# Low parts of the first MLP's w_out: from VectorE to GpSimd, in two pieces

## The chip, the cores and the metric

The kernel runs on one core of one Trainium2 chip. The core has TensorE (matrix multiplication; PE in the profile, its weight loads PEld), VectorE (DVE), ScalarE (ACT), GpSimd (POOL) and SyncE (SP), which here issues the DMAs. They have a queue of instructions each and wait for one another through semaphores. The metric is device time in microseconds, the median of the runs.

## What is computed

Attention with a causal window of 128 over 4 batches, 8 heads, 576 positions and a head dimension of 64; then two MLPs over all 2304 tokens, with a model dimension of 512 and a hidden one of 2048:

```python
scores = where(mask, scale * q @ k.T - slope * distance, -1e9)
x = softmax(scores) @ v                   # tokens x 512
h = x @ w_in                              # 512 x 2048
g = where(h >= 1, h, where(h <= -1, 0, (h + 1) ** 2 / 4))
x = g @ w_out                             # 2048 x 512
h = x @ w_in2
return (h * clip(h + 3, 0, 6) / 6) @ w_out2
```

## The kernel before, in words

The weights lie in memory as 64-bit floating-point numbers. The kernel loads them as pairs of 32-bit words and makes 32-bit numbers of them itself; q, k and v are 32-bit numbers already.

TensorE multiplies in the type fp32r. To keep more digits, most operands are split: a high part, which is the operand cast to fp32r, and a low part, which is the operand less its high part. A product is then three matmuls (low by high, high by low, high by high). split_hi (L135) and split_lo (L143) make the parts, each on the engine that it is given.

The class Weights (L148) holds an MLP's weights in 16 chunks (KF) of 128 hidden columns. A chunk f holds the w_in half (512 columns: four blocks of the model dimension) and the w_out half (512 columns). For each chunk:

- load issues two DMAs, for w_in and for w_out, into raw.
- conv1 (L173): ScalarE makes the tile m from raw (L178, 128x1024) and changes raw in place (L179).
- conv2 (L181): VectorE puts the number together in m: a shift (L185), a combination of sign and rest (L187), an addition (L189).
- conv3 (L191): ScalarE casts m to the high part (L137 in the profile, 128x1024), and VectorE subtracts it from m to make the low part (L144, 128x1024). High and low part lie in hl, with the size [128, 2, 2, 512]: part, then w_in or w_out, then column. hl takes the place of raw.

The tile m comes from the pool conv, which has three buffers. Tiles for an MLP block's results (o1) share them.

conv_tick (L199) takes one step: conv2 and conv3 of chunk n-1, then conv1 of chunk n. The first two ticks lie at the end of the first attention unit; the others are spread over the blocks of the first MLP by the function spread. The tokens are processed in blocks of 256 (the first three) or 384 columns. The order is: block 0 with the first eight chunks (A), block 1 with the same eight, block 0 with the last eight (Z), block 1 with those, and then the other blocks with all sixteen. Between the matmuls of one chunk and the next, the hook places loads, conversions and attention steps. The chunk that a block uses is converted about one chunk ahead in block 0.

For a chunk, Mlp.first (L542) makes h: 12 matmuls with w_in as weights (L549), beginning with w_in's low part. activate (L574) makes g on VectorE, ScalarE and VectorE (L578, L579, L580), casts its high part on ScalarE (L137) and makes its low part on GpSimd (L144, 128x256 for these blocks). Mlp1.second (L585) makes acc from w_out's parts and g: 12 matmuls (L591). It comes two chunks behind (LAG), so that g has time.

The attention's steps stand between these. prep (L293) makes the parts of k on ScalarE and VectorE (kh L303, kl L305) and those of q (qs): in the first three units the high part on GpSimd (L139 in the profile), the low part on GpSimd (L144). Scores are two matmuls (L329), followed by a reduction on VectorE (L350) and an exponential on ScalarE (L353).

The instructions of every engine but SP are put into an order by a planner when the kernel is built: it goes by the order of the program, and by its own estimate of when an instruction can start. SP's order is that of the program. On the chip every queue is worked off in its order.

Of the kernel before, what the change touches and what calls it, by code (L numbers as in the profile page):

```python
# [38 lines left out]
def tile_window_attention_two_mlps(  # L39
# [21 lines left out]
    PIECE = DM  # L61
# [73 lines left out]
    def split_hi(eng, hi, x):  # L135
        if eng == "act":
            nc.scalar.copy(hi, x)  # L137
        elif eng == "pool":
            nc.gpsimd.tensor_scalar(out=hi, in0=x, scalar1=1.0, scalar2=1.0, op0=ALU.mult, op1=ALU.mult)  # L139
        else:  # L140
            engines[eng].tensor_copy(hi, x)

    def split_lo(eng, lo, x, hi):  # L143
        engines[eng].tensor_tensor(out=lo, in0=x, in1=hi.bitcast(F32), op=ALU.subtract)  # L144

    class Weights:  # L148
        def __init__(self, nm, w_in, w_out, pool):
            self.src = {"i": w_in.bitcast(U32), "o": w_out.bitcast(U32)}  # L150
            self.nm, self.pool = nm, pool
            self.raw, self.m, self.hl = {}, {}, {}
            self.n_load = 0
            self.n_conv = 0
# [36 lines left out]
        def conv3(self, f):  # L191
            del self.raw[f]
            m = self.m.pop(f)
            hl = wpool.tile([P, 2, 2, PIECE], F32R, tag=f"w{f}", name=f"w{self.nm}{f}")
            split_hi("act", hl[:, 0], m)
            split_lo("dve", hl[:, 1], m, hl[:, 0])
            self.hl[f] = hl

        def conv_tick(self):  # L199
# [514 lines left out]
    halves = {}  # L714
    thirds = [0, 1, 2]
    W1 = Weights("a", w_in1, w_out1, cpool)
    chunks = Chunks()


# [13 lines left out]
    with ExitStack() as actx:  # L733
        mlp1 = Mlp1(W1, blocks1, rpool, gpool)
        raw = actx.enter_context(tc.tile_pool(name="raw", bufs=2))
# [15 lines left out]
        att.more_loads(1)  # L751
        W1.load()

        n_pre = unit_steps[0] + LAG_D
        for t in range(n_pre):
            att.tick()
            if t % 3 == 0:
                W1.load()
            if t >= n_pre - 2:
                W1.conv_tick()  # L760

        def spread(part, ticks, conv):

            slots = 2 * len(part)
            att0, conv0 = att.t, W1.n_conv

            def hook(f, after):
                k = 2 * (f - part[0]) + after + 1
                W1.load()
                while W1.n_conv < conv0 + min(conv, -(-conv * k // slots)) and W1.conv_tick():  # L770
# [118 lines left out]
```

## Time and profile before

| | before |
|---|---|
| median of 3 runs | 1000.5 us (999.63 to 1001.77) |
| profiled execution | 999.68 us |
| its span, first to last instruction | 997.9 us |
| TensorE matmuls, busy | 968.9 us (97%) |
| TensorE weight loads, busy | 882.8 us (88%) |
| VectorE, busy | 602.9 us (60%) |
| ScalarE, busy | 515.9 us (52%) |
| GpSimd, busy | 259.3 us (26%) |

The shares are means over stages that have different limits: GpSimd has no work after some 530 us, and the first MLP's weights are converted between some 20 and 158 us. A busy matmul row isn't TensorE at its peak, as matmuls overlap and their ends are modelled; the weight loads, one for each matmul, say more. Times in the rows below are counted from the span's start.

### The profile page before, as it was taken

What the parts mean: (1) busy time and instruction counts of PE and PEld (TensorE: products, weight loads), DVE (VectorE), ACT (ScalarE), POOL (GpSimd) and SP (SyncE); (2) the same over time, 40 slices, a digit from 0 to 9 for tenths busy, and PEclk for the clock granted to TensorE, in tenths of its full rate; (3) what the DMA queues carried; (4) which work ended last, traced back from release to release, by engine and by line L of the source; (5) the groups of instructions that cost most, each with busy time, mean ns of one, the idle gap of its engine ahead of it and who ended that gap; (6) DMA issues with size and microseconds to landing.
All of it is one profiled execution on the core that took longest, in us unless ns stands there. A gap on an engine that the chain in (4) does not pass through costs nothing.

```text
span 997.9 us, 16828 instructions
## 1 busy us (share of the span) xinstructions
PE 968.9 (97%) x5748; PEld 882.8 (88%) x5748; DVE 602.9 (60%) x1544; ACT 515.9 (52%) x1260; POOL 259.3 (26%) x403
## 2 busy tenths in 40 slices
PE   7799999999999999999999999999999999999998
PEld 5687888999999998899999999999988888888886
DVE  4889996587678666668764998942242224223222
ACT  5688874567657566656653878522242223222121
POOL 3335454456545555455530000000000000000000
PEclk9899999999999999999999999999999999999999
DMA  5685823223212121222203884000030002001001
GB/s 171 168 258 173 271 66 87 78 67 94 75 42 80 50 80 44 63 59 80 62 12 105 293 277 169 1 1 1 1 106 1 1 1 84 1 1 43 1 1 42
DMA packets 75092, 80.00 MB, mean 80 GB/s; under 512 B 8704, under 2 KB 67072, under 8 KB 75008
## 3 DMA queue, kind: packets, MB, share of 16 engines
q1 hardware_dynamic: 75008, 78.94, 25.8%
q8 instruction: 45, 0.74, 0.3%
q14 instruction: 39, 0.32, 0.1%
HBM read 68.42 MB, written 10.49 MB: 79 GB/s over the span
## 4 chain that ended last, share of the span: by engine, by line
PE 85%; DVE 6%; ACT 4%; issue 2%; DMA 2%; POOL 1%; SPq 0%; ACTq 0%; DVEq 0%; POOLq 0%
PE h L549 37%; PE acc L646 20%; PE acc L591 17%; PE s L329 3%; PE r L466 3%; PE r L411 2%; PE t L380 1%; PE t L381 1%; DVE kl L305 1%; DVE r L578 1%; DMA qr<-qT 1%; ACT p L353 1%; DVE r L580 1%; DVE p L350 1%; DMA vr<-v 1%
## 5 line engine op out<-in xcount | busy, mean ns | idle before, releaser
L549 PE MATMUL h<-x,wa 128*128 128x384 f32 (+1 forms) x1344 | 231.5, 316 | 4.4 <-DVE r L580 2.5
L591 PE MATMUL acc<-g,wa 128*128 128x384 f32 (+1 forms) x1344 | 228.8, 315 | 1.7 <-POOL g L144 1.5
L549 PEld LDWEIGHTS h<-x,wa 128*128 128x128 f32 x1344 | 207.6, 190 | 7.0 <-DVE r L580 4.4
L549 PE MATMUL h<-x,wb 128*128 128x512 f32 (+1 forms) x960 | 210.5, 368 | 0.0
L591 PEld LDWEIGHTS acc<-g,wa 128*128 128x128 f32 x1344 | 206.3, 189 | 4.0 <-POOL g L144 2.2
L646 PE MATMUL acc<-wb,g 128*128 128x512 f32 x864 | 209.4, 390 | 0.0
L549 PEld LDWEIGHTS h<-x,wb 128*128 128x128 f32 x960 | 176.3, 188 | 25.0
L646 PEld LDWEIGHTS acc<-wb,g 128*128 128x128 f32 x864 | 161.7, 188 | 32.3
L636 DVE SCALAR_TENSOR_TENSOR r<-r,h 128x512 f32<-128x512 f32 (+1 forms) x80 | 50.7, 633 | 195.5 <-ACT r L635 195.4
L635 ACT ACTIVATE r<-h 128x512 f32<-128x512 f32 (+1 forms) x80 | 44.4, 556 | 207.9 <-PE h L549 207.8
L137 ACT CAST g<-r 128x384 fp32r<-128x384 f32 (+2 forms) x192 | 98.3, 512 | 69.6 <-DVE r L636 48.7
L144 POOL TENSOR_TENSOR g<-r,g 128x256 fp32r<-128x256 f32 (+1 forms) x96 | 92.0, 958 | 129.2 <-ACT g L137 114.0
L579 ACT ACTIVATE r<-r 128x384 f32<-128x384 f32 (+1 forms) x112 | 53.6, 478 | 93.5 <-DVE r L578 93.3
L353 ACT ACTIVATE p<-p,sm 128x256 f32<-128x256 f32 (+2 forms) x160 | 76.0, 476 | 24.4 <-DVE sm L350 21.6
L144 DVE TENSOR_TENSOR g<-r,g 128x384 fp32r<-128x384 f32 (+1 forms) x96 | 59.9, 624 | 44.7 <-ACT g L137 44.6
L578 DVE TENSOR_SCALAR r<-h 128x384 f32<-128x384 f32 (+1 forms) x112 | 55.5, 496 | 37.4 <-PE h L549 33.2
L144 POOL TENSOR_TENSOR qs<-qr,qs 64x256 fp32r<-64x256 f32 (+3 forms) x88 | 68.8, 781 | 28.4 <-issue 7.5
L580 DVE TENSOR_TENSOR r<-h,r 128x384 f32<-128x384 f32 (+1 forms) x112 | 55.7, 497 | 28.9 <-ACT r L579 28.3
L350 DVE CUSTOM_DVE_ANT_0 p<-s,dist 128x256 f32<-128x256 f32 (+2 forms) x160 | 59.7, 375 | 11.1 <-PE s L329 8.8
L358 POOL TENSOR_SCALAR p<-p,sm 128x256 f32<-128x256 f32 (+1 forms) x104 | 48.1, 463 | 61.7 <-DVE sm L357 37.4
L329 PE MATMUL s<-kh,qs 128*128 128x256 f32 (+2 forms) x160 | 55.0, 347 | 1.8 <-POOL qs L144 1.2
L305 DVE SCALAR_TENSOR_TENSOR kl<-kr,kh 128x256 fp32r<-128x256 f32 (+4 forms) x88 | 51.7, 587 | 7.3 <-ACT kh L303 7.1
(75 smaller groups left out, 1153.5 us busy)
## 6 DMA issues: line engine op xcount, KB each, us to landing
rawa<-w_in SPq DMA_DIRECT2D x16, 512.0 KB, 5.6
rawa<-w_out SPq DMA_DIRECT2D x16, 512.0 KB, 5.1
rawb<-w_in SPq DMA_DIRECT2D x16, 512.0 KB, 3.8
rawb<-w_out SPq DMA_DIRECT2D x16, 512.0 KB, 4.6
kr<-kT SPq DMA_DIRECT2D x80, 64.0 KB, 2.3
out<-o SPq DMA_DIRECT2D x18, 256.0 KB, 2.1
qr<-qT SPq DMA_DIRECT2D x64, 64.0 KB, 2.3
vr<-v SPq DMA_DIRECT2D x24, 128.0 KB, 2.4
```

The costliest lines, as they stand in the source:

```text
L137: nc.scalar.copy(hi, x)
L144: engines[eng].tensor_tensor(out=lo, in0=x, in1=hi.bitcast(F32), op=ALU.subtract)
L305: nc.vector.scalar_tensor_tensor(out=u.kl[:, :nk], in0=u.kr[:, :nk], scalar=unit, in1=u.kh[:, :nk].bitcast(F32), op0=ALU.mult, op1=ALU.sub ...
L329: nc.tensor.matmul(ps[:m, :nk], q[:, qo:qo + m], k[:, ko:ko + nk], start=(w == 0), stop=(w == len(parts) - 1))
L350: nc.vector.tensor_tensor_reduce(out=pt[:m, :nk], in0=ps[:m, :nk], in1=dist[:m, bo:bo + nk], scale=-slopes[u.h], scalar=3.0e38, op0=ALU.ad ...
L353: nc.scalar.activation(out=pt[:m, :nk], in_=pt[:m, :nk], func=AF.Exp, bias=sm[:m, 0:1], scale=-1.0, accum_out=None if u.whole else sm[:m, ...
L549: nc.tensor.matmul(ps[:, :n], self.W.w_in(a, c, f), self.x_chunk(x, b, c, n), start=(k == 0), stop=(k == 3 * KC - 1))
L578: nc.vector.tensor_scalar(out=r[:, :n], in0=ps[:, :n], scalar1=-1.0, scalar2=1.0, op0=ALU.max, op1=ALU.min)
L579: nc.scalar.activation(out=r[:, :n], in_=r[:, :n], func=AF.Square, bias=0.5, scale=0.5)
L580: nc.vector.tensor_tensor(out=r[:, :n], in0=ps[:, :n], in1=r[:, :n], op=ALU.max)
L591: nc.tensor.matmul(acc[i][:, o * n:(o + 1) * n], self.W.w_out(a, f)[:, e * P:(e + 1) * P], g[:, b, :n], start=(first and k == 0 and o == 0 ...
L646: nc.tensor.matmul(acc[t][:, :DM], g[:, b, t * P:(t + 1) * P], self.W.w_out(a, f), start=(first and k == 0), stop=(last and k == 2))
```

## The change

For the first MLP alone (W1.lo_pool = True), conv3 makes the low part in three instructions in place of one. VectorE subtracts only the w_in half, 128x512. GpSimd subtracts the w_out half in two pieces of 128x256. The high part remains one cast on ScalarE. The second MLP's weights are converted as before, and no DMA is changed.

```diff
     class Weights:
+        lo_pool = False
+
         def __init__(self, nm, w_in, w_out, pool):
...
             split_hi("act", hl[:, 0], m)
-            split_lo("dve", hl[:, 1], m, hl[:, 0])
+            if self.lo_pool:
+
+                split_lo("dve", hl[:, 1, 0], m[:, 0], hl[:, 0, 0])
+                for q in range(0, PIECE, PIECE // 2):
+                    cols = slice(q, q + PIECE // 2)
+                    split_lo("pool", hl[:, 1, 1, cols], m[:, 1, cols], hl[:, 0, 1, cols])
+            else:
+                split_lo("dve", hl[:, 1], m, hl[:, 0])
             self.hl[f] = hl
...
     W1 = Weights("a", w_in1, w_out1, cpool)
+    W1.lo_pool = True
     chunks = Chunks()
```

## Rows read from the trace of the kernel before

**Rows 1.** Windows: start:end, length, busy us of each engine (instructions), clock, DMA

```profile
75.00:150.00 75.00, 72.36 (x556) 64.03 (x556) 71.31 (x167) 61.65 (x140) 38.70 (x39) 1.00 0.53 169
175.00:200.00 25.00, 25.00 (x213) 25.00 (x213) 15.00 (x47) 13.59 (x39) 10.90 (x17) 1.00 0.26 78
25.00:160.00 135.00, 124.53 (x921) 108.78 (x920) 123.41 (x301) 106.09 (x249) 61.16 (x64) 0.97 0.59 179
```

**Rows 2.** The chain that ended last, between 75 and 150 us, shares by line

```profile
by line: PE h L549 24.9%; PE acc L591 19.4%; PE r L411 10.6%; issue 5.1%; ACT rawa L179 3.6%; DMA kr<-kT 3.0%; PE s L329 2.9%; PE t L381 2.9%; DMA qr<-qT 2.8%; ACT p L353 2.5%; POOL g L144 2.1%; ACT wa L137 2.0%; PE s L116 1.9%; DVE ma L189
```

**Rows 3.** Groups by line and shape, 25 to 160 us: busy us, mean ns

```profile
L144 DVE TENSOR_TENSOR wa<-ma,wa 128x1024 fp32r<-128x1024 f32 x16 | 20.9, 1304 | 0.9 <-ACT wa L137 0.8
L189 DVE CUSTOM_DVE_ANT_0 ma<-rawa,ma 128x2048 uint16<-128x2048 uint16 x15 | 20.2, 1349 | 0.6 <-ACT rawa L179 0.6
L187 DVE SCALAR_TENSOR_TENSOR ma<-rawa,ma 128x1024 uint32<-128x1024 uint32 x15 | 19.5, 1302 | 0.1
L185 DVE TENSOR_SCALAR ma<-ma 128x1024 uint32<-128x1024 uint32 x15 | 11.8, 786 | 0.8 <-ACT ma L178 0.8
L305 DVE SCALAR_TENSOR_TENSOR kl<-kr,kh 128x448 fp32r<-128x448 f32 x8 | 6.8, 844 | 0.2 <-ACT kh L303 0.2
```

**Rows 4.** The same view, whole span: the second MLP's stage

```profile
L144 DVE TENSOR_TENSOR g<-r,g 128x512 fp32r<-128x512 f32 x48 | 33.2, 692 | 31.0 <-ACT g L137 31.0
...
L144 DVE TENSOR_TENSOR wb<-mb,wb 128x1024 fp32r<-128x1024 f32 x16 | 19.5, 1217 | 0.3 <-ACT wb L137 0.2
L189 DVE CUSTOM_DVE_ANT_0 mb<-rawb,mb 128x2048 uint16<-128x2048 uint16 x16 | 19.5, 1217 | 0.0
L187 DVE SCALAR_TENSOR_TENSOR mb<-rawb,mb 128x1024 uint32<-128x1024 uint32 x16 | 19.4, 1218 | 0.0
...
L185 DVE TENSOR_SCALAR mb<-mb 128x1024 uint32<-128x1024 uint32 x16 | 10.7, 687 | 1.7 <-ACT mb L178 1.6
```

**Rows 5.** Timeline: start, length in us, instruction, [idle before <-releaser]

```profile
40.21 0.62 DVE L305 SCALAR_TENSOR_TENSOR kl<-kr,kh 128x448 fp32r<-128x448 f32 x1
...
52.22 0.87 POOL L144 TENSOR_TENSOR qs<-qr,qs 64x320 fp32r<-64x320 f32 x1
52.26 1.31 DVE L305 SCALAR_TENSOR_TENSOR kl<-kr,kh 128x448 fp32r<-128x448 f32 x1 [0.24 <-ACT kh L303]
...
90.47 2.99 POOL L144 TENSOR_TENSOR qs<-qr,qs 64x192 fp32r<-64x192 f32 x1
```

**Rows 6.** Instructions on the tile g, 25 to 160 us: shortest/median/longest ns

```profile
L144 POOL TENSOR_TENSOR g<-r,g x20: 724/742/1674, 51.0 to 158.9; 128x256 fp32r<-128x256 f32 x20
```

**Rows 7.** Timeline: casts and subtractions of chunks, and a matmul behind one

```profile
22.18 1.04 ACT L137 CAST wa<-ma 128x1024 fp32r<-128x1024 f32 x1 [0.77 <-DVE ma L189]
...
25.27 1.22 DVE L144 TENSOR_TENSOR wa<-ma,wa 128x1024 fp32r<-128x1024 f32 x1
...
94.78 1.22 DVE L144 TENSOR_TENSOR wa<-ma,wa 128x1024 fp32r<-128x1024 f32 x1
...
96.05 1.10 PE L549 MATMUL h<-x,wa 128*128 128x256 f32 x7 [0.60 <-DVE wa L144]
...
154.18 1.05 ACT L137 CAST wa<-ma 128x1024 fp32r<-128x1024 f32 x1 [1.05 <-DVE ma L189]
...
155.25 1.23 DVE L144 TENSOR_TENSOR wa<-ma,wa 128x1024 fp32r<-128x1024 f32 x1
```

**Rows 8.** Timeline: a g on ScalarE and GpSimd, and the next acc

```profile
96.36 0.41 ACT L137 CAST g<-r 128x256 fp32r<-128x256 f32 x1
...
96.91 1.49 POOL L144 TENSOR_TENSOR g<-r,g 128x256 fp32r<-128x256 f32 x1 [3.45 <-ACT g L137]
...
101.94 0.92 PE L591 MATMUL acc<-g,wa 128*128 128x256 f32 x6
```

**Rows 9.** Timeline of ScalarE: a wait for a buffer of m

```profile
136.19 1.17 ACT L178 ACTIVATE ma<-rawa 128x1024 f32<-128x1024 f32 x1 [0.26 <-DVE wa L144]
```

**Rows 10.** Who waited for whom, 25 to 160 us: total us, times, longest

```profile
PE acc L591 <- POOL g L144: 1.5, 3, 0.6
```

## The prediction

> **What bounds the kernel now.** I read four views in turn. First the windows [rows 1]: between 175 and 200 us the weight loads fill the window (25.00 of 25 us), so TensorE sets the time there, and an engine beside it that gets less work would change nothing. Where the first MLP's weights are converted, from 25 to 160 us, it is otherwise. VectorE is busy 71.31 of 75 us between 75 and 150 us, and 123.41 of 135 us over the stretch, while TensorE's weight loads are busy 64.03 of 75 us. So VectorE is the tightest engine there, and TensorE has at most about 11 us to win back between 75 and 150 us. The granted clock of that window is 1.00, so the clock is no term of the sum. GpSimd works 61.16 of 135 us in 64 instructions.
>
> Second, the chain of waits between 75 and 150 us [rows 2]. It runs through TensorE's h and acc for 44% and then through short pieces of ScalarE, VectorE, GpSimd and input DMAs: no engine holds it alone. A microsecond taken off VectorE can shorten the stretch, but not always by a whole one.
>
> Third, the groups of that stretch [rows 3] against the same operations for the second MLP's weights, where GpSimd does nothing [rows 4]. Every conversion operation is dearer in the first place: 1304 against 1217 ns, 1349 against 1217, 1302 against 1218, 786 against 687. Fourth, the timeline shows why [rows 5]: a kl that takes 0.62 us alone took 1.31 us when a GpSimd subtraction had begun 0.04 us earlier, and ended 0.48 us after it; and a GpSimd subtraction took 2.99 us while one VectorE operation with two SBUF inputs followed another. The two engines block each other.
>
> **The change, part by part.** All of it lies between 22 and some 158 us; nothing behind that is edited, and it carries over whatever the stretch gains or loses.
>
> *VectorE loses work.* Sixteen subtractions of 128x1024 become sixteen of 128x512. Without GpSimd beside them these sizes cost 1217 and 692 ns [rows 4], so 0.525 us each goes, 16 x 0.525 = 8.4 us.
>
> *GpSimd gains work.* Thirty-two subtractions of 128x256 with two SBUF inputs. The same shape is its g low part: median 742 ns, shortest 724, longest 1674 [rows 6]; in the mean 997 with what blocks it. So 23.7 us unblocked, 32 us at that mean. GpSimd has 135 - 61 = 74 us without work [rows 1], and the sum fits.
>
> *The two engines collide more.* VectorE's loss to blocking today: 16 x 0.087 + 15 x 0.132 + 15 x 0.084 + 15 x 0.099 = 6.1 us for the conversions [rows 3, 4], and 8 x (0.844 - 0.62) = 1.8 us for the large kl [rows 3, 5]. That is 7.9 us beside 64 GpSimd instructions, 0.123 us for each. Thirty-two more at this rate cost 4.0 us. The new ones are not spread at random, since a piece is released by the same ScalarE cast as VectorE's half. Over the sixteen pairs of cast and subtraction, from 22.18 and 25.27 us to 154.18 and 155.25 us [rows 7], seven subtractions begin within 0.06 us of the cast's end, as the last does (155.23 to 155.25). There VectorE should take the memory first, since a GpSimd subtraction released by a cast begins later than that (after 96.77 at 96.91 us [rows 8]; that cast is at 96.36, 0.41 us long). Seven wait 0.3 to 0.7 us for VectorE itself, as that at 94.78 us. There GpSimd comes first, unless VectorE's operation just before also blocks it, and VectorE can lose up to 0.74 less what it would have waited anyway. Following each pair through its next operations I come to 4.9 us; I take 4.6, between the two. Bounds: nothing, if pieces always fall beside operations that read PSUM; or 32 x 0.742 = 23.7 us, if each holds VectorE for all its length.
>
> VectorE's net relief is then 8.4 - 4.6 = 3.8 us. The bounds are 8.4 us of relief and 15.3 us of loss.
>
> *What of it reaches the end.* The chain passes from engine to engine, and VectorE is busy 91% of the stretch. I take three quarters, 2.85 us. Part of it is direct: the first matmul of a chunk waits for the low part of w_in, which is now ready 0.5 us earlier (at 96.05 us TensorE had stood 0.60 us for it [rows 7]). What is late next in that place is r, the activation, again VectorE's.
>
> *The buffer m is held longer.* It is released when the last subtraction has read it, and GpSimd's two pieces end later than VectorE's 1.2 us did: 2 x 0.74 plus up to 0.7 us behind the other engine, so 0.3 to 1.0 us later. The pool has three buffers, and mostly the next user comes some microseconds after. But at 136.19 us ScalarE had waited 0.26 us for exactly this release [rows 9], and in the order of starts I count one more place like it. Behind that ScalarE instruction stand the next casts of g and exponentials. Two such places at 0.7 us are 1.4 us of ScalarE; I count half, 0.7 us. Nothing to 3 us are the ends.
>
> *GpSimd's queue.* It is in order: behind a waiting piece stand the low parts of g, for which acc waits, and of q, for which the scores wait. TensorE's matmuls waited 1.5 us in three places for g [rows 10]. Usually there is cover: the g that ended at 98.40 us was followed by the next acc at 101.94 us [rows 8], 3.5 us later, because acc runs two chunks behind h. One chunk's pieces, 1.5 us, fit in that. I take zero; without the cover it is 16 x 0.74 = 12 us at most.
>
> No DMA is added or moved, and no step passes SP's queue. The w_out low part itself ends later than before, but is first read two chunks on. Cost zero; the two chunks of matmuls cover it, and if they did not, the whole added 1 us per chunk would show.
>
> **Sum.** -2.85 + 0.7 = -2.15 us against the profiled execution's 999.68 us (span 997.9 and 1.8 around it), which gives 997.5. That execution lies 0.8 us under the median of the runs shown, so 998.3 us. One can tell about 0.2% (2 us) from no change; the forecast sits on that edge.
>
> **Rivals.** *The relief arrives whole:* the pieces fall into VectorE's PSUM reads, and h gets its weights sooner. For it: the seven pairs where VectorE goes first. Against it: every conversion operation already pays today. 8.4 x 0.75 = 6.3 less, 994.2 us.
>
> *It arrives nowhere:* TensorE's attention, ScalarE (106.09 of 135 us) and the q loads take the place of what VectorE gives. For it: the chain's many small pieces. Against it: VectorE's 95% between 75 and 150 us. 1000.5 us.
>
> *The shared port becomes the bound, and it is slower.* An operation that blocks now lasts 0.69 us on VectorE and 1.48 us on GpSimd instead of 1.22 us, 0.95 us more per chunk, 15 us in all. It decides where a piece costs VectorE more than 8.4/32 = 0.26 us, twice today's rate. At 0.45 us: 14.4 - 8.4 = 6.0, three quarters of it 4.5, with the buffer's 0.7 gives 1005.7 us. For it: the 2.99 us subtraction; against: the 0.123 us of today. The Trainium skill has this rule (SBUF — State Buffer, Who interferes with whom): a GpSimd instruction that reads SBUF and a VectorE one with two SBUF inputs exclude each other, and the second to start waits in full. By that rule the trace agrees with 1.31 and 2.99 us; and the bound where each piece blocks in full would be its worst case.
>
> *GpSimd's queue is late:* a piece whose cast is late stands ahead of a ready g or q. It decides when a backlog passes the 3.5 us of cover. Half of the 12 us above, 6.0 - 2.15 = +3.9: 1004.4 us.
>
> **Chances.** Forecast 0.45 (its own range 996 to 1000, a fifth of it within 0.2%), whole relief 0.08, nowhere 0.19, port 0.18, queue 0.10. Faster: 0.36 + 0.08 = 0.44. Same: 0.09 + 0.19 = 0.28. Slower: 0.28. The low end lies under the whole relief, at 993.0; the high end at 1004.0 leaves out the upper half of the port's and queue's cases, about one in seven.
>
> **What would show it.** Right: VectorE's subtraction near 0.7 to 0.9 us with 16 of 128x512 and 32 of 128x256 on GpSimd; the other conversion operations some 0.03 to 0.1 us dearer; VectorE's busy time between 25 and 160 us down by 3 to 5 us; the end of the last conversion some 2 us earlier; everything from 175 us on shifted, not stretched. Wrong: VectorE's busy time not less, matmuls of acc waiting for GpSimd's g for many microseconds, scores waiting for q, or ScalarE waiting for m in more than three places.

## The result: slower, and the profile after

The changed kernel took 1007.8 us (1005.72 to 1008.96, 4 runs) against 1000.3 us before: a ratio of 1.0073 [1.0055, 1.0092]. Run twice more beside experiments it gave 1.0041 [1.0018, 1.0064] and 1.0046 [1.0028, 1.0064]. The forecast was 998.3 us; it is slower by 4 to 7 us. The profiled execution took 1008.96 us, span 1007.2 us.

The windows of the kernel after (start:end, length, busy us of TensorE, its weight loads, VectorE, ScalarE and GpSimd with instructions, granted clock, DMA share, GB/s); the first three are those of [rows 1]:

```profile
75.00:150.00 75.00, 67.59 (x502) 59.27 (x502) 65.91 (x162) 62.20 (x137) 46.54 (x51) 0.98 0.54 170
175.00:200.00 25.00, 25.00 (x213) 25.00 (x212) 13.49 (x43) 12.21 (x34) 10.43 (x16) 1.00 0.36 109
25.00:160.00 135.00, 119.13 (x837) 103.21 (x837) 112.33 (x280) 102.61 (x232) 79.90 (x90) 0.91 0.56 172
25.00:50.00 25.00, 18.91 (x95) 15.48 (x94) 18.11 (x46) 15.77 (x32) 11.21 (x14) 0.66 0.51 150
```

and one window more of the kernel before:

```profile
25.00:50.00 25.00, 19.97 (x124) 16.83 (x122) 21.25 (x51) 17.24 (x39) 8.24 (x10) 0.85 0.61 166
```

VectorE has less work, but TensorE does not get more done for it: 502 matmuls between 75 and 150 us instead of 556, and 837 instead of 921 between 25 and 160 us. Behind 175 us the weight loads fill the window as before, and everything is only shifted.

The granted clock fell with TensorE's work between 25 and 50 us, from 0.85 to 0.66 of full speed (between its levels of 1.2 and 2.4 GHz), and part of the loss goes with the clock. Over the whole span its mean was 0.991 in 149 executions of the kernel before and 0.988 in 24 of the changed kernel. Those of the kernel before took 1000.5 us in the mean at 0.993 or more, and 1006.2 us at 0.984 to 0.986. At a like clock (0.990 to 0.992, 0.987 to 0.989, 0.984 to 0.986) the changed kernel is 4.4, 1.9 and 2.5 us longer, where all executions together give 5.1 us. Whether the lower clock costs the rest, or only comes with TensorE's waits, is not shown.

The groups of the kernel after, 25 to 170 us (busy us, mean ns; the counterpart of [rows 3]):

```profile
L191 DVE CUSTOM_DVE_ANT_0 ma<-rawa,ma 128x2048 uint16<-128x2048 uint16 x16 | 20.7, 1294 | 0.1
L189 DVE SCALAR_TENSOR_TENSOR ma<-rawa,ma 128x1024 uint32<-128x1024 uint32 x15 | 20.4, 1361 | 0.1
L144 DVE TENSOR_TENSOR wa<-ma,wa 128x512 fp32r<-128x512 f32 x16 | 14.9, 931 | 0.2 <-ACT wa L137 0.2
L187 DVE TENSOR_SCALAR ma<-ma 128x1024 uint32<-128x1024 uint32 x15 | 11.0, 734 | 0.0
...
L314 DVE SCALAR_TENSOR_TENSOR kl<-kr,kh 128x448 fp32r<-128x448 f32 x8 | 7.3, 911 | 0.2
L144 POOL TENSOR_TENSOR wa<-ma,wa 128x256 fp32r<-128x256 f32 x32 | 30.0, 955 | 32.5 <-ACT wa L137 15.2 <-issue 11.2 <-DVE y L440 3.6
```

VectorE's subtraction takes 0.931 us, not the undisturbed 0.692. The last row is new: ahead of its 32 pieces GpSimd stood idle for 32.5 us, 15.2 us of it for ScalarE's casts. The waits of the kernel after, 25 to 170 us (who for whom, total us, times, longest), tell who paid:

```profile
POOL wa L144 <- ACT wa L137: 15.2, 5, 4.2
...
PE s L338 <- POOL qs L144: 8.9, 6, 2.7
```

and of the kernel before (20 to 175 us):

```profile
PE s L329 <- POOL qs L144: 1.2, 1, 1.2
```

TensorE's scores wait 8.9 us for q instead of 1.2. No matmul of acc waits for g any more [rows 10]. One such place, in the timeline of the kernel after (start, length, [idle before <-releaser]):

```profile
141.97 1.97 POOL L144 TENSOR_TENSOR wa<-ma,wa 128x256 fp32r<-128x256 f32 x2 [1.55 <-ACT wa L137]
143.92 0.79 POOL L139 TENSOR_SCALAR qs<-qr 128x192 fp32r<-128x192 f32 x1
144.61 1.12 ACT L180 ACTIVATE ma<-rawa 128x1024 f32<-128x1024 f32 x1 [0.89 <-DVE wa L144]
144.68 0.73 POOL L144 TENSOR_TENSOR g<-r,g 128x256 fp32r<-128x256 f32 x1
145.49 0.59 POOL L144 TENSOR_TENSOR qs<-qr,qs 64x192 fp32r<-64x192 f32 x1
...
146.13 0.33 PE L338 MATMUL s<-kh,qs 128*128 128x128 f32 x1 [2.68 <-POOL qs L144]
```

GpSimd stands 1.55 us for the cast, with a high part of q behind the two pieces. Pieces, q's high part, a g and q's low part then follow without a gap, and TensorE has stood 2.68 us when the scores begin. In the same place ScalarE waited 0.89 us for a buffer of m; VectorE's own subtraction released it, not the two pieces, which had ended before.

### The profile page after: what moved, and what is told of

Its sections match the earlier page's. It is cut to its first block, busy times and chain, and to the rows that moved or that the text cites. A ratio compares the mean times of both kernels' runs of the same rounds, so it can differ in the third digit from the quotient of the medians.

```text
span 1007.2 us, 16886 instructions
## 1 busy us (share of the span) xinstructions
PE 976.2 (97%) x5748; PEld 889.5 (88%) x5748; DVE 599.4 (60%) x1545; ACT 516.1 (51%) x1259; POOL 284.0 (28%) x435
## 4 chain that ended last, share of the span: by engine, by line
PE 79%; DVE 6%; issue 4%; ACT 3%; POOL 3%; DMA 3%; SPq 1%; POOLq 0%; ACTq 0%; DVEq 0%
PE h L558 36%; PE acc L655 20%; PE acc L600 16%; PE r L475 2%; PE s L338 2%; DMA qr<-qT 1%; SPq L272 1%; PE t L389 1%; PE t L390 1%; POOL g L144 1%; DVE kl L314 1%; PE r L420 1%; DMA vr<-v 1%; POOL wa L144 1%; POOL qs L144 1%
## 5 line engine op out<-in xcount | busy, mean ns | idle before, releaser
L558 PEld LDWEIGHTS h<-x,wa 128*128 128x128 f32 x1344 | 210.6, 193 | 4.6 <-DVE r L589 2.6
L144 POOL TENSOR_TENSOR qs<-qr,qs 64x256 fp32r<-64x256 f32 (+3 forms) x88 | 65.7, 746 | 24.8 <-issue 7.5
L314 DVE SCALAR_TENSOR_TENSOR kl<-kr,kh 128x256 fp32r<-128x256 f32 (+4 forms) x88 | 53.9, 612 | 7.4 <-ACT kh L312 6.9
```

Of the source, the lines that this page charges most:

```text
L314: nc.vector.scalar_tensor_tensor(out=u.kl[:, :nk], in0=u.kr[:, :nk], scalar=unit, in1=u.kh[:, :nk].bitcast(F32), op0=ALU.mult, op1=ALU.sub ...
L558: nc.tensor.matmul(ps[:, :n], self.W.w_in(a, c, f), self.x_chunk(x, b, c, n), start=(k == 0), stop=(k == 3 * KC - 1))
```

## The experiments

All of them change Weights.conv3 or where its pieces are queued. In the runs of the relief, of small pieces, of unread pieces and of fills, the low parts of w_out's half are not made, and acc's matmuls read the low parts of w_in's half in their place (expectations that say "high parts" there are mistaken in the word):

```
-            return self.hl[f][:, part, 1, :]
+            return self.hl[f][:, part, 0 if part and self.lo_pool else 1, :]
```

The planner gives the other engines a new order with the change: in the traces, 450 of TensorE's 5748 matmuls stand at another place than before. With the relief alone it is 452, and these two orders differ in only 80 places, so the new order is not what costs. The runs of small pieces, of unread pieces at held places or behind q, and of fills at those places have the relief's order on VectorE, ScalarE and for GpSimd's other work, and on TensorE but for at most 10 places; the fills in place differ from it in 172.

**The relief alone**; run twice.

```
-                for q in range(0, PIECE, PIECE // 2):
-                    cols = slice(q, q + PIECE // 2)
-                    split_lo("pool", hl[:, 1, 1, cols], m[:, 1, cols], hl[:, 0, 1, cols])
```

> VectorE makes the w_in half of the low part alone (128x512); nobody makes the w_out half, and acc reads w_in's low part in its place, so TensorE's work is the same and GpSimd gets none. Queue theory (GpSimd's pieces stand in its queue ahead of q's parts, and the scores wait): faster than before, 994 to 999 us, TensorE waits for q no longer than before. Port theory (GpSimd's added time in memory blocks VectorE): the same, 994 to 999 us. Planner theory (the new order of the other engines' instructions is what costs): still 1004 us or more, although GpSimd has no more work than before.

> Left out: as in the first run of the relief alone (VectorE makes w_in's half, nobody w_out's, the second products of acc read w_in's high parts). The base of the run beside it on the same chip: 996 to 1000 us, a ratio of 0.993 to 0.997.

998.23 us, ratio 0.9946 [0.9926, 0.9965], and 997.58 us, 0.9949 [0.9928, 0.997]: 5.3 us faster. The relief is real; 8.4 us taken off VectorE give 0.63 of that. (The medians lie 3.5 and 3.3 us under those of the kernel before beside them, so the share is uncertain.) TensorE waits 3.1 and 3.6 us for q here, more than before the change: with these 3 us the other runs are to be compared.

**The pieces behind q.** The change whole, but each pair is queued behind the next low part of q, or at the next conversion:

```
+                self.flush_late()
+                self.late.append(late)
...
+            ins = split_lo(LO["q"], u.qs[D:, :m], u.qr[D:, :m], u.qs[D:, :m])
+            with tc.issue_after(ins.ins):
+                W1.flush_late()
```

> The changed kernel with one edit: each chunk's two pieces are put into GpSimd's queue behind the next q low part (or at the next chunk's conversion, if none comes before). Same work on both engines. Queue theory: TensorE's waits for q fall from 8.9 us to under 3 us and the time to 996 to 1001 us. Port theory: the blocking is the same, 1005 to 1009 us. Planner theory: not told apart, anything from 998 to 1008 us.

1014.58 us, ratio 1.0114 [1.0075, 1.0152]: a miss, and slower than the change. The waits of this run:

```profile
ACT ma L185 <- POOL wa L144: 5.0, 2, 3.9
PE s L348 <- POOL qs L144: 4.9, 5, 1.6
```

q is late less, but the pieces hold m longer, and ScalarE now waits for the buffer, once for 3.9 us. The granted clock of these four executions was 0.981 to 0.983, lower than in any of the change's 24.

**One piece per chunk** of 128x512 instead of two:

```
-                for q in range(0, PIECE, PIECE // 2):
-                    cols = slice(q, q + PIECE // 2)
-                    split_lo("pool", hl[:, 1, 1, cols], m[:, 1, cols], hl[:, 0, 1, cols])
+                split_lo("pool", hl[:, 1, 1], m[:, 1], hl[:, 0, 1])
```

> The changed kernel with the w_out half as one GpSimd subtraction of 128x512 in place of two of 128x256. Queue theory: q stands behind the same length of work and the same wait for the cast, 1006 to 1010 us. Port theory: one longer hold of the memory instead of two, VectorE's blocked operations lose up to 1.4 us at once, 1008 to 1014 us. Planner theory: another order, anything from 1000 to 1010 us.

1007.29 us, 1.0054 [1.0033, 1.0075]: as the change. That there are two pieces costs nothing.

**Load without a wait, first try.** The pieces read high parts of the chunk before, unread by anyone:

```
+                if f:
+                    old = self.hl[f - 1]
+                    for q in range(0, PIECE, PIECE // 2):
+                        cols = slice(q, q + PIECE // 2)
+                        split_lo("pool", old[:, 1, 1, cols], old[:, 0, 1, cols].bitcast(F32), old[:, 0, 0, cols])
```

> VectorE makes the w_in half alone and acc reads w_in's low part for w_out's, as in the run with the relief alone (0.9946 of before, -5.4 us). GpSimd gets thirty 128x256 subtractions of the same length and kind at the same places in its queue, but on the two high halves of the chunk converted before, written where nobody reads: they never wait for the cast, and they don't hold m. Theory that the wait at the queue's head does it: the wait is gone, 997 to 1001 us. Theory that the load does it (the pieces' own time, in the queue and in the memory that VectorE needs): 1003 to 1008 us, TensorE still waiting for q.

1005.63 us, 1.0038 [1.0012, 1.0064]. It does not test what it was built for: the planner moved the pieces up to right behind that chunk's cast, and GpSimd still waited 14.3 us for wa from ScalarE, TensorE 9.7 us for q. But that makes it the change without the hold of m. TensorE, VectorE and ScalarE have the change's order in every place; in GpSimd's queue one g and one q have changed places, and the last chunk's pieces are missing. Against the change's 1.0041 to 1.0073, the hold is worth 0.3 to 3.5 us (1.5 to 2.2 us between the medians).

**The wait without load.** The change's pieces with 8 columns each; run twice.

```
-                    cols = slice(q, q + PIECE // 2)
+                    cols = slice(q, q + 8)
```

> The counterpart: the same relief, and GpSimd's thirty-two subtractions read m and the cast as in the changed kernel and stand at the same places in its queue, but have 8 columns in place of 256, written where nobody reads. They wait for the cast and then take next to no time. Wait theory: 1002 to 1007 us, TensorE waits for q 5 us or more. Load theory: 995 to 999 us, like the relief alone.

> Left out: as beside it. Two pieces of 8 columns per chunk, which wait for the cast, and no fills: the base on the same chip, 999 to 1002 us.

1000.38 us, 0.999 [0.9966, 1.0013], and 1000.49 us, 0.9987 [0.9969, 1.0005]: 4 us above the relief by the ratios, 2.5 us by the medians, with the same order on every engine. TensorE waits 6.1 and 5.9 us for qs instead of 3.1 and 3.6. The traced executions themselves (998.6 and 999.9 us, against 999.2 and 998.3 with the relief) do not show the loss; it rests on all the executions, 22 against 20. GpSimd is busy 11.8 us with these pieces (206 ns in the median, up to 1067 where VectorE is in the way), and stood 28.6 and 30.5 us ahead of them.

**The load at held places**, ahead of q: the unread pieces, each kept in program order, so that they cannot move up to the cast:

```
+                        tc.keep_in_program_order(split_lo(
+                            "pool", old[:, 1, 1, cols], old[:, 0, 1, cols].bitcast(F32), old[:, 0, 0, cols]))
```

> Left out: the low parts of w_out's half are not made, the second products of acc read the high parts of w_in in their place; GpSimd makes 30 pieces of 128x256 out of high parts of the chunk before, which were ready some 9 us earlier, into a place that nobody reads, at places of its queue that are now held fixed, so that they cannot move up behind a cast. So GpSimd has nearly the load of the change without its wait for the cast and without holding m. If q is late because pieces stand in GpSimd's queue and wait for ScalarE's casts, nearly all of the loss goes: 999 to 1001 us, GpSimd waits for wa under 3 us in all (32 with the change), TensorE waits for qs 1 to 4 us (8.9). If it is the pieces' own time (0.7 to 1 us each, ahead of q and on the memory beside VectorE), it stays near the run whose pieces had moved up (1005.6): 1003 to 1007 us, with TensorE's waits for qs still 6 to 9 us.

1010.18 us, 1.0079 [1.0051, 1.0106]. My theory of that moment, that the loss is only the wait for the cast, falls: GpSimd waited for no cast here, and TensorE waits longest of all:

```profile
PE s L341 <- POOL qs L144: 11.3, 7, 3.0
```

**Late chunks only**, nothing left out, with the change beside it:

```
-            if self.lo_pool:
+            if self.lo_pool and f >= 8:
```

> Nothing is left out: the change for chunks 8 to 15 alone; VectorE makes both halves of chunks 0 to 7 in one instruction as before. If the loss is spread over the pieces alike, half of it: 1003 to 1005 us. If most of it comes from the early stretch (25 to 75 us, where the granted clock fell from .85 to .66 in 25 to 50 us), the late chunks alone cost nothing or gain half of the relief: 997 to 1001 us, with a clock of .83 to .87 in 25 to 50 us.

> The changed kernel itself, as a base for the two others on the same chip: 1005 to 1009 us, a ratio of 1.005 to 1.009.

1003.92 us, 1.0019 [0.9995, 1.0043], against 1.0041 for the change. Half the pieces, about half the loss: it is not the early stretch's alone, as far as the intervals tell.

**The unread pieces behind q**: the same pieces at the places of the run that queued the change's pieces there:

```
+                self.flush_late()
+                if f:
+                    def late(old=self.hl[f - 1]):
...
+                    self.late.append(late)
```

> Left out: the low parts of w_out's half (the second products of acc read the high parts of w_in in their place). GpSimd makes 30 pieces of 128x256 from the chunk before, unread, as in the run before it whose pieces stood ahead of q, but each pair is queued behind the next low part of q, or at the next conversion. Every other instruction of every engine stands in the order of the run of the relief alone, so only the place of the pieces differs. If the pieces cost because they stand ahead of q in GpSimd's queue (the run with them ahead: 1010 us, TensorE waiting 11.3 us for qs), most of it goes: 998 to 1002 us, TensorE's waits for qs 2 to 5 us. If it is the memory, on which GpSimd's 30 us of pieces and VectorE's instructions stand in each other's way wherever they are, 1004 to 1010 us, with VectorE's conversions and kl as long as there or longer.

1005.66 us, 1.0035 [1.0011, 1.0058]: between both theories' numbers. 8.6 us of it remain over the relief although TensorE waits only 5.2 us for qs. In the traced execution g was late too, once, behind two pieces that lasted 3.27 us together (a line of the timeline and one of the waits):

```profile
151.84 3.27 POOL L144 TENSOR_TENSOR wa<-wa 128x256 fp32r<-128x256 f32 x2
...
PE acc L611 <- POOL g L144: 2.8, 1, 2.8
```

**Time without reading.** At the places of the last run, and at the held places ahead of q (there kept in program order again), GpSimd fills the unread place with zeros:

```
+                    for _ in range(3):
+                        nc.gpsimd.memset(old[:, 1, 1].bitcast(F32), 0.0)
```

> Left out: the low parts of w_out's half (the second products of acc read w_in's high parts). At the places of GpSimd's queue where the run of the load without a cast to wait for had its pieces, ahead of q, GpSimd now fills the unread place with zeros, three times 128x512 per chunk. By the fills in the trace of before (206 ns for 128 columns, 99 ns for 1) that should be 1.6 us per chunk, about the 1.5 us of two undisturbed pieces, but with nothing read from memory. If the pieces cost because they occupy GpSimd ahead of q: 1004 to 1009 us, TensorE waiting 8 us or more for qs. If they cost because GpSimd and VectorE keep each other off the memory: 997 to 1001 us, TensorE's waits for qs 3 to 5 us, and VectorE's instructions as long as with the relief alone.

> Left out: as in the run beside it. The same fills at the places behind q's low parts, where the subtractions gave 1005.7 us against 997.6 of the relief alone. If time on GpSimd costs wherever it stands: 1002 to 1006 us. If it is the memory: 996 to 999 us, as the relief alone. If only a place ahead of q costs, this one is at 996 to 999 us too and the run beside it at 1004 to 1009 us.

1000.95 us, 0.998 [0.9963, 0.9998], and 1000.15 us, 0.9975 [0.9962, 0.9988]. The groups of the run with fills ahead of q, 20 to 170 us, have

```profile
L204 POOL MEMSET wa<- 128x512 f32 x45 | 24.6, 546 | 1.6
```

and those of the run with unread pieces behind q

```profile
L144 POOL TENSOR_TENSOR wa<-wa 128x256 fp32r<-128x256 f32 x30 | 34.0, 1154 | 3.7 <-ACT wa L137 2.8
```

25 us of GpSimd's time that read nothing cost about 3 us, wherever they stand. Subtractions there, 8 to 9 us longer in all (32.9 us ahead of q, 34.0 behind it; 30 x 0.742 = 22.3 us undisturbed), cost 6 us more behind q and 10 us more ahead of it. VectorE's instructions lengthen with them: summed over conversions and all kl, beyond their undisturbed lengths, 13.4 us behind q against 8.2 with fills. The Trainium skill says (SBUF — State Buffer, Who interferes with whom) that VectorE with two SBUF inputs contends with a GpSimd instruction that reads SBUF, not with one that only writes it. These runs agree: with fills VectorE lost 6.3 and 8.2 us, with the relief alone 7.5 and 7.4.

**The change, built up in place.** At the change's own places: a piece of 8 columns that waits for the cast, three fills; then the same with a last piece of 8 columns, which holds m until then.

```
+                cols = slice(0, 8)
+                split_lo("pool", hl[:, 1, 1, cols], m[:, 1, cols], hl[:, 0, 1, cols])
+                for _ in range(3):
+                    nc.gpsimd.memset(hl[:, 1, 1].bitcast(F32), 0.0)
+                split_lo("pool", hl[:, 1, 1, cols], m[:, 1, cols], hl[:, 0, 1, cols])
```

> Left out: the low parts of w_out's half (the second products of acc read w_in's high parts). Per chunk GpSimd makes at the change's own places a piece of 8 columns, which waits for the cast, then three fills of 128x512 (0.55 us each in the fills before), then a piece of 8 columns again, which holds m until then. So the wait for the cast, the hold of m and the time on GpSimd are those of the change; only the reading of two operands of 256 columns is gone. If the change's loss is above all waits and GpSimd's time: within 2 us of the changed kernel beside it, 1003 to 1008 us. If it is above all the two engines on the memory: 4 to 7 us below it, 999 to 1002 us.

> The changed kernel, as the base on the same chip: 1004 to 1008 us, a ratio of 1.004 to 1.007.

> Left out: the low parts of w_out's half (the second products of acc read w_in's high parts). As the fill in place (1006.6 us), but without the last piece of 8 columns: the first one waits for the cast, three fills of 128x512 follow, and m is free again behind the first. If the hold of m is a small term, as the prediction's 0.7 us: 1005 to 1007 us. If the hold makes up what the wait alone (1000.4 us) and the fills alone (3 us more than the relief) leave: 1001 to 1003.5 us.

1006.61 us, 1.0059 [1.0036, 1.0082], with the change beside it at 1007.58 us, 1.0046; and without the last piece 1002.41 us, 1.0012 [1.0, 1.0025]. The second small piece reads m and is the later wait in GpSimd's queue as well: with it TensorE waits 6.2 us for qs instead of 3.6, and ScalarE 1.6 us for m instead of none. So these 4.7 us are not the hold's price alone.

The run without the last piece lost part of its time early, at a low clock. Its window, and that of the second run of small pieces:

```profile
25.00:50.00 25.00, 21.47 (x98) 18.50 (x98) 17.55 (x47) 16.41 (x32) 9.19 (x18) 0.57 0.62 175
...
25.00:50.00 25.00, 19.02 (x115) 16.42 (x115) 19.82 (x52) 17.62 (x37) 10.46 (x19) 0.80 0.62 183
```

TensorE was busy longer with fewer matmuls, so there it was slower and did not wait more. Between 75 and 150 us the two come to 535 and 544 matmuls, though GpSimd has its fills in every chunk.

The steps, with 0.001 of the ratio as 1.0 us (the clock is the mean of all executions):

| what GpSimd does for w_out's half | ratio | median, us | clock | step, us |
|---|---|---|---|---|
| nothing, VectorE relieved | 0.9946, 0.9949 | 998.2, 997.6 | 0.992, 0.992 | -5.3 |
| two pieces of 8 columns, which wait for the cast | 0.9990, 0.9987 | 1000.4, 1000.5 | 0.991, 0.991 | +4.1 |
| one such piece, then three fills | 1.0012 | 1002.4 | 0.988 | +2.4 |
| the unread pieces that had moved up: wait, time and two operands read, m not held | 1.0038 | 1005.6 | 0.988 | +2.6 |
| the change itself | 1.0073, 1.0041, 1.0046 | 1007.8, 1007.1, 1007.6 | 0.987, 0.987, 0.989 | +0.3 to +3.5 |

The first two rows have one order on TensorE, the last two another, and the third a third; and the clock falls with the third. So the wait's step and the hold's are each taken within one order, and the two between them are less sure. The time on GpSimd is better priced by the fills in the relief's own order: about 3 us. The intervals leave each step some 2 to 3 us either way.

Nor does the fill with a last piece (1.0059), as slow as the change, show that the collisions are free. It occupied GpSimd more than the change did (fills 25.2 us and small pieces 13.1 us, against 30.0):

```profile
L204 POOL MEMSET wa<- 128x512 f32 x48 | 25.2, 526 | 2.3
...
L144 POOL TENSOR_TENSOR wa<-ma,wa 128x8 fp32r<-128x8 f32 x32 | 13.1, 408 | 22.7 <-ACT wa L137 10.2 <-issue 9.6 <-POOL qs L144 1.4
```

## Why the prediction was wrong

*VectorE loses work: right.* 16 subtractions of 128x512 and 32 pieces of 128x256 are there. *What of it reaches the end: about right*, 0.63 measured by the ratios (0.4 by the medians), three quarters taken; -5.3 us instead of -6.3 for a relief without collisions.

*The two engines collide more: right in VectorE's own count, wrong as the whole price.* By the prediction's way of counting, on the rows after: 16 x (0.931 - 0.692) + 15 x (1.361 - 1.218) + 16 x (1.294 - 1.217) + 15 x (0.734 - 0.687) + 8 x (0.911 - 0.62) = 3.8 + 2.1 + 1.2 + 0.7 + 2.3 = 10.1 us, against 7.9 before: +2.2 us, with the smaller kl +3.9, where 4.6 was taken. But it counts VectorE alone. A collision also lengthens GpSimd's side, 0.955 us a piece against 0.742, and where q is behind, TensorE waits for that: away from the change's places, reading two operands cost 6 to 10 us of the end more than filling; at the change's own places the step is 2.6 us.

*The buffer m is held longer: not refuted.* 0.7 us was taken with 3 us as the end; the change without the hold gives 0.3 to 3.5 us for it. ScalarE's direct waits for m were 1.3 us in the change, 0.4 us of it for GpSimd's pieces. Behind q, where the pieces let go of m later, the term grows: those that read m came to 1.0114, the unread ones to 1.0035, 7.9 us less (their orders differ in 287 of TensorE's places, and the clock was lower).

*GpSimd's queue: this is the step that failed.* "I take zero" rested on the 3.5 us that g has until the next acc. The cover was real, and acc did not wait. But the same sentence named q, and q has no such cover: its scores come next, and the kernel before already waited 1.2 us for it. In the change TensorE waited 8.9 us. The wait for the cast, with the small pieces' own time, costs 4.1 us (2.5 by the medians), and the time on GpSimd about 3 us: 7 us where nothing was put, inside the 12 us given as the end. With the relief, -5.3 + 4.1 + 3 = +1.8 us; measured were +4.1 to +7.3, and what is left, 2.3 to 5.5 us, falls to the reading of two operands and the hold.

*The clock: put at no term*, because [rows 1] has 1.00 between 75 and 150 us. The same rows have 0.97 from 25 to 160 us, and with the change the two were 0.98 and 0.91. Some 1 to 3 of the 5 us go with it; whether it causes them stays open.

The rival "GpSimd's queue is late" (1004.4 us) had the mechanism, "a piece whose cast is late stands ahead of a ready g or q", and a tenth of the chance; but its condition, a backlog beyond g's 3.5 us, was not needed, since q has less cover. The shared port as the bound (1005.7 us) had the time nearer, but not its condition: a piece cost VectorE about 0.07 to 0.12 us, not more than 0.26. VectorE's busy time between 25 and 160 us fell by 11 us instead of 3 to 5 above all because work had slipped out of that window (280 instructions instead of 301), not for the relief.

No version that does all the work came out ahead of the kernel before: the 5.3 us of relief are less than the wait, the time on GpSimd, the collisions and the hold together.

## What to carry to other kernels

Before work goes to an engine with free time, read that engine's queue: for every kind of instruction behind the new one, how long its consumer can wait, and take the one with the least cover, not the best covered. An instruction that waits for another engine hands that wait to its whole queue, even if it does almost nothing itself. Price the new user of a buffer by when it lets go of it. And when a stretch's clock is given as full, look at the windows beside it too.

## What the runs showed that was not expected

- 32 GpSimd pieces of 8 columns, 0.388 us each in the mean, made the kernel 4.1 us slower than no pieces by the ratios, 2.5 us by the medians.
- Three fills of 128x512 per chunk (0.53 to 0.58 us each) cost about 3 us, and 30 subtractions of 128x256 at the same places 9 to 13 us over the relief; VectorE's instructions were 4.6 to 5.2 us longer in all beside the subtractions than beside the fills.
- Within one kernel, executions at a lower mean clock are longer: 1000.5 us at 0.993 or more, 1006.2 us at 0.984 to 0.986, in the kernel before.
- A run with a clock of 0.57 between 25 and 50 us was busy 21.47 us for 98 matmuls there; one with 0.80 was busy 19.02 us for 115.
